# Retention scores as plain float32 products on halves and quarters of TensorE's array, with TensorE's order written by hand

## The chip, the cores and the metric

The kernel runs on one core of one Trainium2 chip. The metric is the time of one execution on the device, in microseconds (us); lower is better. Three runs of the kernel before were timed. A further execution was recorded by the hardware profiler, and all rows of the profile come from that one.

The engines by their names in the profile: PE is TensorE's matmul and PEld its weight load, DVE is VectorE, ACT is ScalarE, POOL is GpSimd, SP is SyncE, which here only issues transfers (its queue is SPq). L309 is line 309 of the kernel.

## The reference

Two stages follow each other: a causal retention over 8 batches of 576 tokens with 8 heads of width 64, and a layer of 8 experts in which each token goes to one.

```python
scores = scale * np.matmul(q, k.transpose(0, 1, 3, 2))
gamma = 1.0 - 2.0 ** (-5.0 - np.arange(H, dtype=np.float32))
rel = pos[:, None] - pos[None, :]
Dmat = np.where(rel >= 0, gamma[:, None, None] ** rel[None, :, :], 0.0)
attn = np.matmul(scores * Dmat[None], v)          # [8, 8, 576, 64]
x = attn.transpose(0, 2, 1, 3).reshape(4608, 512)
...
logits = x @ w_gate
e_idx = np.argmax(logits, axis=1)
for e in range(8):                                # only the tokens with e_idx == e
    h = np.maximum(x[mask] @ w1[e], 0.0)          # 512 -> 1024
    out[mask] = gate_w * eom * (h @ w2[e])        # 1024 -> 512
```

The largest logit decides the expert, so the retention's result has to be nearly exact float32.

## The kernel before, in words

The 4608 tokens are 36 tiles of 128. Nine tiles cover two batches, so the fifth of nine (c == 4) holds the end of one batch and the start of the next. Retention runs over these tiles with a running state: powers of gamma are multiplied into v (`vp`, on GpSimd) and into the output (`gq_sb`), so that the masked scores of a tile need only a mask of ones and zeros, and all earlier tiles of the batch enter through a state of 64x64 per head.

An iteration g of the main loop holds:

- `load`: one transfer of 1 MB brings q and k transposed, and k and v in natural order, into one of three buffers (`pk`). It is issued two tiles ahead, once the buffer is free.
- `update`: four matmuls over pairs of heads add this tile's k'v to `st_ps` (the two diagonal 64x64 blocks of a pair's 128x128 result are wanted), and ScalarE copies the diagonal blocks into `stbd`, whose other blocks are zero.
- `prep` for the next tile: `kh` (k cast to float32r, ScalarE) and `kl` (the difference, GpSimd), `qh` (two casts into block-diagonal arrays, ScalarE); `prep_ql` makes `ql` (two differences, VectorE).
- `scores`: per pair of heads three float32r products, kh'qh + kh'ql + kl'qh, each 128x128 by 128x256 over the block-diagonal q (L309). VectorE multiplies by the mask into `S_sb` (L311). The first tile alone (FP = 1) takes plain float32 products of 64 rows (L305).
- `xnat` of the tile before: four matmuls turn `xT` into natural order and give the gate logits in the same pass (L432); ScalarE copies x out, and SP writes it to `xs` in memory. After every fourth tile `gate1` runs the gating operations on VectorE and `gate2` ranks the tokens by two small matmuls; GpSimd then scatters slots into `lst`.
- `outT`: the state's product with q (L342, pairs of heads, block-diagonal state), then the values' product with `S_sb` (L347, one head at a time, 64 columns of the array), into `o_ps`; VectorE scales it into `xT` (L352).

The weights of expert 0 are loaded and cast in this loop too (`load_w`, L129 to L138). Near the end of the loop the first 384 slots of expert 0 are read and their tokens gathered and transposed; then the expert pass starts with `mm1` (L192) and goes on with `mm2` (L207) in an order written out by hand. In the retention loop a scheduler orders the instructions of each engine. Each engine runs its own list in that order and waits at semaphores for the others. PSUM has eight banks; here the scores have two tiles of two banks each.

Of the kernel before, what the change touches and what calls it, by code (L numbers as in the profile page):

```python
# [13 lines left out]
I32 = mybir.dt.int32  # L14
# [20 lines left out]
KB = DM // P  # L35
FB = F // P
GT = 4                      # tiles of a gating group
FP = 1                      # first tiles, whose scores are plain float32 products
NOV = 40                    # most overflow tiles
# [3 lines left out]
def tile_retention_moe(  # L43
# [44 lines left out]
    lists = const.tile([P, E, CT * 4, 2], I32, name="lists")   # (quadrant, j): slots of all column blocks  # L88
    idx = const.tile([P, E, CT, 2], I32, name="idx")           # by token column
    gidx = const.tile([P, E, CT * 4], I32, name="gidx")        # rows of a quarter of a token  # L90
# [4 lines left out]
    qbd = [[const.tile([P, NP, 2, P], F32R, name=f"q{x}{i}") for x in "hl"] for i in range(2)]  # L95
    stbd = [const.tile([P, NP, P], F32, name=f"stbd{i}") for i in range(2)]
# [50 lines left out]
    def gather_rows(e, t, rows):  # L147
        # From the first rows alone: an empty slot's index is beyond them and leaves its zeros.
        x = xg.tile([P, DM], F32, name="x_g")
        V.memset(x, 0.0)  # L150
        G.indirect_dma_start(out=x, out_offset=None, in_=xs[0:rows, :],
                             in_offset=bass.IndirectOffsetOnAxis(ap=idx[:, e, t, 0:1], axis=0),
                             bounds_check=rows - 1, oob_is_err=False)
        XG[e, t] = x

    def gather(e, t, u):
        # Quarter rows of 32 tokens, quarter a in partitions 32a on.
        if u == 0:
            XG[e, t] = pools["xq"].tile([P, 4, P], F32, name="x_q")
        G.indirect_dma_start(out=XG[e, t][:, u, :], out_offset=None, in_=xs.rearrange("t (a c) -> (t a) c", a=4),  # L160
                             in_offset=bass.IndirectOffsetOnAxis(ap=gidx[:, e, 4 * t + u:4 * t + u + 1], axis=0))
# [71 lines left out]
    actx = ExitStack()  # L233
    ld = actx.enter_context(tc.tile_pool(name="ld", bufs=3, side="right"))
# [3 lines left out]
    ps_s = psctx.enter_context(tc.tile_pool(name="ps_s", bufs=2, space=PSUM, side="right"))  # L238

    pk, ks, vs, xT, gt = {}, {}, {}, {}, {}  # L240
# [26 lines left out]
    def prep(g):  # L267
        c = g % CPB
        q = pk[g][:, 0].rearrange("p (a i) -> p a i", a=NP)
        k = pk[g][:, 1].rearrange("p (a i) -> p a i", a=NP)  # L270
        vp = wk.tile([P, H, D], F32, name="vp")
        vs[g] = vp
        if g < FP:
            G.tensor_tensor(out=vp, in0=pk[g][:, 3].rearrange("p (h d) -> p h d", h=H),
                            in1=gk_sb[:, c].broadcast_to([P, H, D]), op=ALU.mult)
            return
        kh = wk.tile([P, NP, P], F32R, name="kh")
        kl = wk.tile([P, NP, P], F32R, name="kl")
        A.copy(out=kh, in_=k)  # L279
        G.tensor_tensor(out=kl, in0=k, in1=kh.bitcast(F32), op=ALU.subtract)  # L280
        G.tensor_tensor(out=vp, in0=pk[g][:, 3].rearrange("p (h d) -> p h d", h=H),  # L281
                        in1=gk_sb[:, c].broadcast_to([P, H, D]), op=ALU.mult)
        ks[g] = (kh, kl)
        qh = qbd[g % 2][0]
        for r in range(2):
            s = slice(64 * r, 64 * r + 64)
            A.copy(out=qh[s, :, r, :], in_=q[s])  # L287

    def prep_ql(g):
        q = pk[g][:, 0].rearrange("p (a i) -> p a i", a=NP)  # L290
        qh, ql = qbd[g % 2]
        for r in range(2):
            s = slice(64 * r, 64 * r + 64)
            V.tensor_tensor(out=ql[s, :, r, :], in0=q[s], in1=qh[s, :, r, :].bitcast(F32), op=ALU.subtract)  # L294

    def scores(g):
        c = g % CPB
        sc = [ps_s.tile([P, 2, 2, P], F32, name=f"s{i}") for i in range(2)]
        S_sb = wk.tile([P, NP, 2, P], F32, name="S_sb", bufs=1)
        m = cmat_sb[:, 2 if c == 4 else 1, :, :].broadcast_to([P, 4, P])  # L300
        for p in range(NP):
            if g < FP:
                for r in range(2):
                    q, k = (pk[g][64 * r:64 * r + 64, i, P * p:P * p + P] for i in range(2))
                    T.matmul(sc[r][:, p // 2, p % 2], lhsT=k, rhs=q, start=True, stop=True)  # L305
                continue
            (kh, kl), (qh, ql) = ks[g], qbd[g % 2]
            for j, (a, b) in enumerate(((kh, qh), (kh, ql), (kl, qh))):
                T.matmul(sc[p // 2][:, p % 2], lhsT=a[:, p, :], rhs=b[:, p], start=(j == 0), stop=(j == 2))  # L309
        for i in range(2):  # L310
            V.tensor_tensor(out=S_sb[:, :, i] if g < FP else  # L311
                            S_sb[:, 2 * i:2 * i + 2].rearrange("p a r i -> p (a r) i"),
                            in0=sc[i].rearrange("p a r i -> p (a r) i"), in1=m, op=ALU.mult)
        return S_sb

    def update(g):
        c = g % CPB
        if c == 8:
            return
        if c in (0, 4):  # L320
            st_ps[0] = ps_1.tile([P, NP, P], F32, name="st_ps")
        lo = 64 if c == 4 else 0
        kn = pk[g][:, 2].rearrange("p (a i) -> p a i", a=NP)
        vv = vs[g].rearrange("p (a r) d -> p a (r d)", a=NP)
        for p in range(NP):
            T.matmul(st_ps[0][:, p, :], lhsT=kn[lo:P, p, :], rhs=vv[lo:P, p, :],
                     start=(c in (0, 4) and p == 0), stop=True, skip_group_check=True)
        s = stbd[g % 2]
        for r in range(2):
            q = slice(64 * r, 64 * r + 64)  # L330
            A.copy(out=s[q, :, q], in_=st_ps[0][q, :, q])
        stcur[0] = s

    def outT(g, S_sb, state):
        c = g % CPB
        o = ps_1.tile([P, NP, P], F32, name="o_ps")
        first = True
        q = pk[g][:, 0].rearrange("p (a i) -> p a i", a=NP)
        if state is not None:
            w = 64 if c == 4 else P  # L340
            for p in range(NP):
                T.matmul(o[:, p, 0:w], lhsT=state[:, p, :], rhs=q[:, p, 0:w],  # L342
                         start=first, stop=False, skip_group_check=True)
                first = False
        for p in range(NP):
            for r in range(2):
                T.matmul(o[64 * r:64 * r + 64, p, :], lhsT=vs[g][:, 2 * p + r, :],  # L347
                         rhs=S_sb[:, p, r, :], start=(state is None and p == 0), stop=True,
                         skip_group_check=True)
        x = wk.tile([P, NP, P], F32, name="xT", bufs=1)  # L350
        c0 = P * c if c < 5 else 64 + P * (c - 5)
        V.tensor_tensor(out=x, in0=o, in1=gq_sb[:, :, c0:c0 + P], op=ALU.mult)  # L352
# [40 lines left out]
    def gate2(ps, fresh):  # L393
# [20 lines left out]
        if n == SNAP:  # L414
            # Expert 0's first CA slots are read from here on: later tokens take slots from CA up.
# [36 lines left out]
    for t in stbd:  # L452
        V.memset(t, 0.0)
    for t in qbd[1] + qbd[0]:
        V.memset(t.bitcast(F32), 0.0)
    # The array's clock rises with work: zeros, while the first tile is on its way.
    warm = ps_1.tile([P, 512], F32, name="xa")
    for n in (512, 512, 256):
        T.matmul(warm[:, 0:n], lhsT=stbd[0][:, 0, :], rhs=stbd[0].rearrange("p a c -> p (a c)")[:, 0:n],
                 start=True, stop=True)  # L460
    prep(0)
    for g in range(NTILE):
        c = g % CPB
        if 0 < g < NTILE - 2:
            load(g + 2)
        prev = stcur[0] if c != 0 else None
        update(g)
        if g + 1 < NTILE:
            prep(g + 1)
        S_sb = scores(g)  # L470
# [4 lines left out]
        if FP <= g + 1 < NTILE:  # L475
            prep_ql(g + 1)
        outT(g, S_sb, prev)
        if g % 4 == 3 and g // 4 < 8:
            load_w(1 + (g // 4) % 2, 0, g // 8)
    psctx.close()  # L480
# [204 lines left out]
```

## Time and profile before

| | |
|---|---|
| time, median of 3 runs | 715.23 us (713.0 to 722.73) |
| span of the profiled execution | 718.8 us |
| instructions | 11429 |
| PE / PEld busy | 662.3 us (92%) / 598.4 us (83%) |
| DVE busy | 444.6 us (62%) |
| ACT busy | 226.3 us (31%) |
| POOL busy | 333.6 us (46%) |
| bytes moved | 103.60 MB, mean 144 GB/s |
| first L192 matmul (start of the expert pass) | 261.9 us |

The profiled execution's own time outside the profiler's span isn't among the numbers; its span is all that is used of it. The span runs from the first instruction to the last. A row of groups gives line, engine, operation, output and inputs, shapes and count, then the busy time, the mean duration in ns, and the idle time of the engine just ahead of it with what ended it. A row in order of time gives start, duration, engine, line and operation, and the count that was merged. In the table of stretches stand the stretch, its length, busy us and count of each engine, the granted clock of TensorE (1.00 is full), the mean busy share of the 16 DMA engines and GB/s.

### The profile page before, as it was taken

To read this page: it belongs to the slowest core of one execution; us is meant where nothing else is said; L and a number is where in the kernel's file an instruction comes from. 1 tells how busy PE (TensorE), PEld (TensorE's weight loads), DVE (VectorE), ACT (ScalarE), POOL (GpSimd) and SP (SyncE) were. 2 spreads that over 40 slices of the span, in tenths; PEclk is the share of its full clock that TensorE was granted. 3 is DMA by queue.
4 is the path that set the end of the run, shared out by engine and by line. 5 is a ranking of instruction groups with operands and counts; after the bars stand their busy time and mean duration, and the time that the engine had idled before them with its cause. 6 is when DMAs were issued, how large, how long until landed. Compare 5 with 4: busy or idle time off the path is not lost. (4 is left out here: it accounts for less than half of the span.)

```text
span 718.8 us, 11429 instructions
## 1 busy us (share of the span) xinstructions
PE 662.3 (92%) x4346; PEld 598.4 (83%) x4346; DVE 444.6 (62%) x836; ACT 226.3 (31%) x476; POOL 333.6 (46%) x305
## 2 busy tenths in 40 slices
PE   7988978798868799889999999999999999999996
PEld 5977877687767699769989989989989989988984
DVE  7778889997856862476765734744753753743500
ACT  4545554553434331222122222222222222222211
POOL 3353635644526423776716715724724733831011
PEclk9988999999989899999999999999999999999998
DMA  9867879758555511454513523622622722721000
GB/s 305 285 172 241 195 281 238 209 201 213 115 181 158 196 46 17 161 164 149 183 65 114 188 78 100 199 77 71 219 78 74 220 70 63 229 74 49 23 31 37
DMA packets 36762, 103.60 MB, mean 144 GB/s; under 512 B 10320, under 2 KB 13777, under 8 KB 32482
## 3 DMA queue, kind: packets, MB, share of 16 engines
q1 hardware_dynamic: 26946, 81.83, 37.6%
q0 software_dynamic: 9328, 19.98, 8.4%
q10 hardware_dynamic: 432, 1.05, 0.4%
q8 instruction: 35, 0.57, 0.4%
q14 instruction: 21, 0.17, 0.1%
HBM read 83.62 MB, written 20.26 MB: 145 GB/s over the span
## 5 line engine op out<-in xcount | busy, mean ns | idle before, releaser
L160 POOL DMA_INDIRECT x_q<-xs,gidx x148 | 167.8, 1134 | 54.8 <-issue 39.6
L192 PE MATMUL h_ps<-xh,w1h 128*128 128x384 f32 (+1 forms) x512 | 156.8, 307 | 4.4 <-DVE hl L195 3.0
L192 PE MATMUL h_ps<-xl,w1h 128*128 128x384 f32 (+1 forms) x512 | 157.0, 307 | 0.8 <-DVE xl L179 0.7
L192 PE MATMUL h_ps<-xh,w1l 128*128 128x384 f32 (+1 forms) x512 | 156.5, 306 | 0.0
L207 PE MATMUL y_ps<-w2h,hh 128*128 128x512 f32 x320 | 124.8, 390 | 1.5 <-ACT hh L194 1.5
L207 PE MATMUL y_ps<-w2h,hl 128*128 128x512 f32 x320 | 126.1, 394 | 0.0
L207 PE MATMUL y_ps<-w2l,hh 128*128 128x512 f32 x320 | 125.2, 391 | 0.0
L211 POOL DMA_INDIRECT out_dram<-y,idx x40 | 40.4, 1009 | 177.7 <-ACT y L210 161.0
L195 DVE SCALAR_TENSOR_TENSOR hl<-h_ps,hh 128x384 fp32r<-128x384 f32 (+1 forms) x128 | 60.6, 487 | 88.3 <-ACT hh L194 88.1
L194 ACT ACTIVATE hh<-h_ps 128x384 fp32r<-128x384 f32 (+1 forms) x128 | 55.8, 440 | 151.3 <-PE h_ps L192 148.9
L192 PEld LDWEIGHTS h_ps<-xh,w1h 128*128 128x128 f32 x512 | 96.0, 188 | 5.9 <-DVE hl L195 3.4
L192 PEld LDWEIGHTS h_ps<-xl,w1h 128*128 128x128 f32 x512 | 96.1, 188 | 1.8 <-DVE xl L179 1.5
L192 PEld LDWEIGHTS h_ps<-xh,w1l 128*128 128x128 f32 x512 | 96.1, 188 | 0.0
L294 DVE TENSOR_TENSOR ql<-pk,qh 64x512 fp32r<-64x512 f32 x70 | 69.3, 990 | 15.1 <-ACT qh L287 13.9
L179 DVE TENSOR_TENSOR xl<-x_t,xh 128x512 fp32r<-128x512 f32 x37 | 25.6, 692 | 75.9 <-ACT xh L178 75.9
L207 PEld LDWEIGHTS y_ps<-w2h,hh 128*128 128x128 f32 x320 | 60.1, 188 | 14.8 <-ACT hh L194 1.9
L207 PEld LDWEIGHTS y_ps<-w2l,hh 128*128 128x128 f32 x320 | 60.1, 188 | 13.5
L207 PEld LDWEIGHTS y_ps<-w2h,hl 128*128 128x128 f32 x320 | 60.1, 188 | 12.8 <-DVE hl L195 0.5
L347 PE MATMUL o_ps<-S_sb,vp 128*64 128x128 f32 x576 | 47.8, 299 | 24.5 <-DVE S_sb L311 24.4
L280 POOL TENSOR_TENSOR kl<-pk,kh 128x512 fp32r<-128x512 f32 x35 | 46.6, 1333 | 50.5 <-ACT kh L279 50.3
L210 ACT ACTIVATE y<-y_ps,idx 128x512 f32<-128x512 f32 x40 | 27.5, 688 | 129.8 <-issue 73.0
L281 POOL TENSOR_TENSOR vp<-pk,gk_sb 128x512 f32<-128x512 f32 x35 | 37.8, 1080 | 55.0 <-PE o_ps L347 23.7
(115 smaller groups left out, 1014.8 us busy)
## 6 DMA issues: line engine op xcount, KB each, us to landing
pk<-in_pack_dram SPq DMA_DIRECT2D x33, 1024.0 KB, 8.2
st<-in_w_dram SPq DMA_DIRECT2D x64, 512.0 KB, 4.2
xs<-x SPq DMA_DIRECT2D x36, 256.0 KB, 3.2
x_q<-xs,gidx POOLq DMA_INDIRECT x148, 3.3
pk<-in_pack_dram SPq DMA_DIRECT2D x3, 512.0 KB, 5.0
gq_sb<-in_gq_dram SPq DMA_DIRECT2D x5, 256.0 KB, 6.9
out_dram<-y,idx POOLq DMA_INDIRECT x40, 2.7
lst<-meta,sli POOLq DMA_INDIRECT x36, 5.8
```

The source lines that it names most:

```text
L160: G.indirect_dma_start(out=XG[e, t][:, u, :], out_offset=None, in_=xs.rearrange("t (a c) -> (t a) c", a=4), in_offset=bass.IndirectOffsetO ...
L179: V.tensor_tensor(out=lo, in0=src, in1=hi.bitcast(F32), op=ALU.subtract)
L192: T.matmul(ps, lhsT=a[:, k, :], rhs=b[:, k, :], start=(j == 0), stop=(j == 3 * KB - 1))
L194: A.activation(out=hh, in_=ps, func=AF.Relu)
L195: V.scalar_tensor_tensor(out=hl, in0=ps, scalar=0.0, in1=hh.bitcast(F32), op0=ALU.max, op1=ALU.subtract)
L207: T.matmul(ps, lhsT=a[:, n], rhs=b, start=(j == 0), stop=(j == 3 * FB - 1))
L210: A.activation(out=y, in_=ps, func=AF.Copy, scale=idx.bitcast(F32)[:, e, t, 1:2])
L211: G.indirect_dma_start(out=out, out_offset=bass.IndirectOffsetOnAxis(ap=idx[:, e, t, 0:1], axis=0), in_=y, in_offset=None, bounds_check=NT ...
L280: G.tensor_tensor(out=kl, in0=k, in1=kh.bitcast(F32), op=ALU.subtract)
L281: G.tensor_tensor(out=vp, in0=pk[g][:, 3].rearrange("p (h d) -> p h d", h=H), in1=gk_sb[:, c].broadcast_to([P, H, D]), op=ALU.mult)
L294: V.tensor_tensor(out=ql[s, :, r, :], in0=q[s], in1=qh[s, :, r, :].bitcast(F32), op=ALU.subtract)
L347: T.matmul(o[64 * r:64 * r + 64, p, :], lhsT=vs[g][:, 2 * p + r, :], rhs=S_sb[:, p, r, :], start=(state is None and p == 0), stop=True, sk ...
```

## The change

q and k are no longer split, and the block-diagonal arrays are gone. Scores are plain float32 products for all tiles, 64 rows of the array per head, the two heads of a pair into two banks. The state is kept as 64x64 blocks per head (`stT`); the state's product with q uses a quarter of the array per head, and the update uses 64 columns. The output's layout over partitions and banks changes with it, so the columns of x come in another order (`SLOT`); gate weights, w1 and `gq` are permuted to match ahead of the launch. There are four input buffers in place of three, three score banks used one at a time by two tiles, and two buffers for `S_sb`. TensorE's order in the loop is the order of the program text: scores of the next tile, `xnat` of the one before, `outT`, then `update`.

```diff
-FP = 1                      # first tiles, whose scores are plain float32 products
+SLOT = [[2 * (2 * (k % 2) + (c - k // 2) % 2) + k // 2 for c in range(2)] for k in range(4)]
...
-    qbd = [[const.tile([P, NP, 2, P], F32R, name=f"q{x}{i}") for x in "hl"] for i in range(2)]
-    stbd = [const.tile([P, NP, P], F32, name=f"stbd{i}") for i in range(2)]
+    zw = const.tile([P, 512], F32, name="zw")
+    stT = [const.tile([P, NP, D], F32, name=f"stT{i}") for i in range(2)]
...
-    ld = actx.enter_context(tc.tile_pool(name="ld", bufs=3, side="right"))
+    ld = actx.enter_context(tc.tile_pool(name="ld", bufs=4, side="right"))
...
-    ps_s = psctx.enter_context(tc.tile_pool(name="ps_s", bufs=2, space=PSUM, side="right"))
+    ps_s = psctx.enter_context(tc.tile_pool(name="ps_s", bufs=3, space=PSUM, side="right"))
...
     def prep(g):
...
-        kh = wk.tile([P, NP, P], F32R, name="kh")
-        kl = wk.tile([P, NP, P], F32R, name="kl")
-        A.copy(out=kh, in_=k)
-        G.tensor_tensor(out=kl, in0=k, in1=kh.bitcast(F32), op=ALU.subtract)
...
-            A.copy(out=qh[s, :, r, :], in_=q[s])
-
-    def prep_ql(g):
...
-            V.tensor_tensor(out=ql[s, :, r, :], in0=q[s], in1=qh[s, :, r, :].bitcast(F32), op=ALU.subtract)
+        vs[g] = wk.tile([P, H, D], F32, name="vp")
+        G.tensor_tensor(out=vs[g], in0=pk[g][:, 3].rearrange("p (h d) -> p h d", h=H),
+                        in1=gk_sb[:, g % CPB].broadcast_to([P, H, D]), op=ALU.mult)
 
     def scores(g):
-            for j, (a, b) in enumerate(((kh, qh), (kh, ql), (kl, qh))):
-                T.matmul(sc[p // 2][:, p % 2], lhsT=a[:, p, :], rhs=b[:, p], start=(j == 0), stop=(j == 2))
+        sc = [ps_s.tile([P, NP, P], F32, name="sc") for _ in range(2)]
+        S_sb = wk.tile([P, 2, NP, P], F32, name="S_sb")
+        for p in range(NP):
+            for r in range(2):
+                q, k = (pk[g][64 * r:64 * r + 64, i, P * p:P * p + P] for i in range(2))
+                T.matmul(sc[r][:, p], lhsT=k, rhs=q, start=True, stop=True)
         for r in range(2):
+            V.tensor_tensor(out=S_sb[:, r], in0=sc[r], in1=m, op=ALU.mult)
 
     def update(g):
-            st_ps[0] = ps_1.tile([P, NP, P], F32, name="st_ps")
+            st_ps[0] = ps_1.tile([P, NP, D], F32, name="st_ps")
         for p in range(NP):
-            T.matmul(st_ps[0][:, p, :], lhsT=kn[lo:P, p, :], rhs=vv[lo:P, p, :],
-                     start=(c in (0, 4) and p == 0), stop=True, skip_group_check=True)
-        s = stbd[g % 2]
-        for r in range(2):
-            q = slice(64 * r, 64 * r + 64)
-            A.copy(out=s[q, :, q], in_=st_ps[0][q, :, q])
+            for r in range(2):
+                o = P * p + 64 * r
+                T.matmul(st_ps[0][64 * r:64 * r + 64, p, :], lhsT=pk[g][lo:P, 2, o:o + D], rhs=vs[g][lo:P, 2 * p + r, :],
+                         start=(c in (0, 4) and p == 0), stop=True, skip_group_check=True)
+        A.copy(out=stT[g % 2], in_=st_ps[0])
 
     def outT(g, S_sb, state):
-        o = ps_1.tile([P, NP, P], F32, name="o_ps")
+        o = ps_s.tile([P, 2, 512], F32, name="o_ps", bufs=1)
+        part = lambda p, r: o[64 * ((p + r) % 2):64 * ((p + r) % 2) + 64, r, P * (p // 2):P * (p // 2) + P]
+        order = [(p, (p + i) % 2) for p in range(NP) for i in range(2)]
         if state is not None:
             w = 64 if c == 4 else P
-            for p in range(NP):
-                T.matmul(o[:, p, 0:w], lhsT=state[:, p, :], rhs=q[:, p, 0:w],
-                         start=first, stop=False, skip_group_check=True)
+            for p, r in order:
+                s = slice(64 * r, 64 * r + 64)
+                T.matmul(part(p, r)[:, 0:w], lhsT=state[s, p, :], rhs=pk[g][s, 0, P * p:P * p + w],
+                         start=(p < 2), stop=False, skip_group_check=True)
+        for p, r in order:
+            T.matmul(part(p, r), lhsT=vs[g][:, 2 * p + r, :], rhs=S_sb[:, r, p, :],
+                     start=(state is None and p < 2), stop=True, skip_group_check=True)
...
     prep(0)
+    pe_order = tc.manual_schedule(engines={mybir.EngineType.PE})
+    pe_order.__enter__()
+    S_next = scores(0)
     for g in range(NTILE):
-        if 0 < g < NTILE - 2:
-            load(g + 2)
-        prev = stcur[0] if c != 0 else None
-        update(g)
+        S_sb = S_next
+        prev = stcur[0] if g % CPB != 0 else None
+        if g < NTILE - 3:
+            load(g + 3)
         if g + 1 < NTILE:
             prep(g + 1)
-        S_sb = scores(g)
+            S_next = scores(g + 1)
...
         if g > 0:
             xnat(g - 1)
-        if FP <= g + 1 < NTILE:
-            prep_ql(g + 1)
         outT(g, S_sb, prev)
+        update(g)
         if g % 4 == 3 and g // 4 < 8:
             load_w(1 + (g // 4) % 2, 0, g // 8)
+    pe_order.__exit__(None, None, None)
```

More of the change, by code (lines that the diff above doesn't have):

```diff
@@ L237, in tile_retention_moe @@
     ps_1 = p1ctx.enter_context(tc.tile_pool(name="ps_1", bufs=1, space=PSUM))
-    ps_s = psctx.enter_context(tc.tile_pool(name="ps_s", bufs=2, space=PSUM, side="right"))
-    pk, ks, vs, xT, gt = {}, {}, {}, {}, {}
+    ps_s = psctx.enter_context(tc.tile_pool(name="ps_s", bufs=3, space=PSUM, side="right"))
+    pk, vs, xT, gt = {}, {}, {}, {}
     st_ps, stcur = [None], [None]
@@ L267, in prep @@
     def prep(g):
[L268 to L276, printed above, removed]
-        kh = wk.tile([P, NP, P], F32R, name="kh")
-        kl = wk.tile([P, NP, P], F32R, name="kl")
@@ L279, in prep @@
[L279 to L284, printed above, removed]
-        for r in range(2):
-            s = slice(64 * r, 64 * r + 64)
-            A.copy(out=qh[s, :, r, :], in_=q[s])
-    def prep_ql(g):
-        q = pk[g][:, 0].rearrange("p (a i) -> p a i", a=NP)
-        qh, ql = qbd[g % 2]
-        for r in range(2):
-            s = slice(64 * r, 64 * r + 64)
-            V.tensor_tensor(out=ql[s, :, r, :], in0=q[s], in1=qh[s, :, r, :].bitcast(F32), op=ALU.subtract)
@@ L296, in scores @@
[L296 to L300, printed above, removed]
-        for p in range(NP):
[L302 to L307, printed above, removed]
-            for j, (a, b) in enumerate(((kh, qh), (kh, ql), (kl, qh))):
[L309 to L313, printed above, removed]
+        vs[g] = wk.tile([P, H, D], F32, name="vp")
@@ new lines, in prep, with scores @@
+        G.tensor_tensor(out=vs[g], in0=pk[g][:, 3].rearrange("p (h d) -> p h d", h=H),
+                        in1=gk_sb[:, g % CPB].broadcast_to([P, H, D]), op=ALU.mult)
+    def scores(g):
+        sc = [ps_s.tile([P, NP, P], F32, name="sc") for _ in range(2)]
+        S_sb = wk.tile([P, 2, NP, P], F32, name="S_sb")
+        m = cmat_sb[:, 2 if g % CPB == 4 else 1, :, :].broadcast_to([P, NP, P])
+        for p in range(NP):
+            for r in range(2):
+                q, k = (pk[g][64 * r:64 * r + 64, i, P * p:P * p + P] for i in range(2))
+                T.matmul(sc[r][:, p], lhsT=k, rhs=q, start=True, stop=True)
+        for r in range(2):
+            V.tensor_tensor(out=S_sb[:, r], in0=sc[r], in1=m, op=ALU.mult)
@@ L320, in update @@
         if c in (0, 4):
-            st_ps[0] = ps_1.tile([P, NP, P], F32, name="st_ps")
+            st_ps[0] = ps_1.tile([P, NP, D], F32, name="st_ps")
         lo = 64 if c == 4 else 0
-        kn = pk[g][:, 2].rearrange("p (a i) -> p a i", a=NP)
-        vv = vs[g].rearrange("p (a r) d -> p a (r d)", a=NP)
         for p in range(NP):
-            T.matmul(st_ps[0][:, p, :], lhsT=kn[lo:P, p, :], rhs=vv[lo:P, p, :],
-                     start=(c in (0, 4) and p == 0), stop=True, skip_group_check=True)
@@ L328, in update @@
-        s = stbd[g % 2]
-        for r in range(2):
-            q = slice(64 * r, 64 * r + 64)
-            A.copy(out=s[q, :, q], in_=st_ps[0][q, :, q])
-        stcur[0] = s
+            for r in range(2):
[3 more added lines that the diff above has]
+        A.copy(out=stT[g % 2], in_=st_ps[0])
@@ L334, in outT @@
+        stcur[0] = stT[g % 2]
     def outT(g, S_sb, state):
         c = g % CPB
-        o = ps_1.tile([P, NP, P], F32, name="o_ps")
-        first = True
-        q = pk[g][:, 0].rearrange("p (a i) -> p a i", a=NP)
+        o = ps_s.tile([P, 2, 512], F32, name="o_ps", bufs=1)
+        part = lambda p, r: o[64 * ((p + r) % 2):64 * ((p + r) % 2) + 64, r, P * (p // 2):P * (p // 2) + P]
+        order = [(p, (p + i) % 2) for p in range(NP) for i in range(2)]
         if state is not None:
             w = 64 if c == 4 else P
-            for p in range(NP):
-                T.matmul(o[:, p, 0:w], lhsT=state[:, p, :], rhs=q[:, p, 0:w],
-                         start=first, stop=False, skip_group_check=True)
-                first = False
@@ L345, in outT @@
[L345 to L349, printed above, removed]
+            for p, r in order:
+                s = slice(64 * r, 64 * r + 64)
+                T.matmul(part(p, r)[:, 0:w], lhsT=state[s, p, :], rhs=pk[g][s, 0, P * p:P * p + w],
+                         start=(p < 2), stop=False, skip_group_check=True)
@@ L350, in outT @@
+        for p, r in order:
+            T.matmul(part(p, r), lhsT=vs[g][:, 2 * p + r, :], rhs=S_sb[:, r, p, :],
+                     start=(state is None and p < 2), stop=True, skip_group_check=True)
         x = wk.tile([P, NP, P], F32, name="xT", bufs=1)
         c0 = P * c if c < 5 else 64 + P * (c - 5)
-        V.tensor_tensor(out=x, in0=o, in1=gq_sb[:, :, c0:c0 + P], op=ALU.mult)
+        V.tensor_tensor(out=x.rearrange("p (r s) i -> p r s i", r=2),
+                        in0=o[:, :, 0:2 * P].rearrange("p r (s i) -> p r s i", s=2),
+                        in1=gq_sb[:, :, c0:c0 + P].rearrange("p (r s) i -> p r s i", r=2), op=ALU.mult)
@@ L451, in tile_retention_moe @@
     load_first()
[L452 to L455, printed above, removed]
+    V.memset(zw, 0.0)
     warm = ps_1.tile([P, 512], F32, name="xa")
     for n in (512, 512, 256):
-        T.matmul(warm[:, 0:n], lhsT=stbd[0][:, 0, :], rhs=stbd[0].rearrange("p a c -> p (a c)")[:, 0:n],
-                 start=True, stop=True)
+        T.matmul(warm[:, 0:n], lhsT=zw[:, 0:P], rhs=zw[:, 0:n], start=True, stop=True)
     prep(0)
+    pe_order = tc.manual_schedule(engines={mybir.EngineType.PE})
+    pe_order.__enter__()
+    S_next = scores(0)
     for g in range(NTILE):
-        c = g % CPB
-        if 0 < g < NTILE - 2:
-            load(g + 2)
-        prev = stcur[0] if c != 0 else None
-        update(g)
+        S_sb = S_next
+        prev = stcur[0] if g % CPB != 0 else None
+        if g < NTILE - 3:
+            load(g + 3)
         if g + 1 < NTILE:
             prep(g + 1)
-        S_sb = scores(g)
+            S_next = scores(g + 1)
         if g < 4:
@@ L634, in _consts @@
     gqh = gam[:, None] ** s[None, :] / np.sqrt(D)
-    gq = np.repeat(gqh.reshape(NP, 2, 1, 640), D, axis=2).reshape(NP, P, 640).transpose(1, 0, 2)
+    gq = np.repeat(gqh[np.array(SLOT)][:, :, None], D, axis=2).reshape(NP, P, 640).transpose(1, 0, 2)
     pos = (np.arange(CPB)[None, :] * P + np.arange(P)[:, None]) % S
@@ L666 @@
     tr = lambda a: nat(a).reshape(NTILE, P, NP, P).transpose(0, 3, 2, 1).reshape(NTILE, P, DM)
+    perm = (np.array(SLOT).reshape(-1, 1) * D + np.arange(D)).reshape(-1)
     arrays = {
         "pack": np.ascontiguousarray(np.stack([tr(q), tr(k), nat(k), nat(v)], axis=2)),
-        "wg": np.concatenate([inputs["moe_w_gate"], inputs["moe_w_output_gate"]], axis=1),
-        "w1": np.ascontiguousarray(np.asarray(inputs["moe_w1"]).reshape(E, P, KB, 4, 256)
+        "wg": np.ascontiguousarray(np.concatenate([inputs["moe_w_gate"], inputs["moe_w_output_gate"]], axis=1)[perm]),
+        "w1": np.ascontiguousarray(np.asarray(inputs["moe_w1"])[:, perm].reshape(E, P, KB, 4, 256)
                                    .transpose(0, 3, 1, 2, 4).reshape(E, 4, P, KB * 256)),
```

## The prediction

> **What bounds the kernel now.** I read the page's head first, then the table of busy time by stretches, then the list of waits, then the order of time of single tiles.
>
> ```profile
> span 718.8 us, 11429 instructions
> core 0: us, PE busy (x) PEld busy (x) DVE busy (x) ACT busy (x) POOL busy (x), PEclk, DMA share, GB/s
> 0.00:40.00 40.00, 34.69 (x292) 29.67 (x292) 29.65 (x69) 20.83 (x44) 15.16 (x20) 1.00 0.88 305
> 40.00:120.00 80.00, 67.31 (x561) 61.51 (x560) 65.89 (x138) 39.72 (x85) 39.02 (x35) 0.89 0.76 205
> 120.00:200.00 80.00, 68.11 (x584) 61.57 (x585) 70.16 (x153) 36.13 (x81) 39.28 (x34) 0.94 0.70 196
> 200.00:264.00 64.00, 50.90 (x423) 46.55 (x423) 44.66 (x117) 26.01 (x61) 28.16 (x25) 0.89 0.47 159
> 320.00:718.80 398.80, 391.05 (x2208) 354.58 (x2206) 206.85 (x299) 92.27 (x181) 179.78 (x160) 1.00 0.34 109
> ...
> L192 PEld LDWEIGHTS h_ps<-xh,w1h x40: 186/188/190, 261.9 to 299.9; 128*128 128x128 f32 x40
> ...
> 9.73 0.33 SPq L245 DMA_DIRECT2D pk<-in_pack_dram  x1
> ...
> 235.49 0.33 SPq L245 DMA_DIRECT2D pk<-in_pack_dram  x1
> ...
> DMA to landing us min/median/max: 4.9/8.2/12.0
> ...
> ACT kh L279 <- DMA pk<-in_pack_dram: 49.7, 18, 7.2
> PE o_ps L347 <- DVE S_sb L311: 24.4, 16, 5.6
> ```
>
> The expert pass is TensorE alone (391 of 399 us busy, full clock), and the change does not touch it. Its first product (L192) starts at 261.9, so what the change can move is the time of that start, the handover. Before it no engine is full: TensorE has gaps, its granted clock falls to 0.89, and VectorE and the DMA engines are half to nine tenths busy. What sets the pace is a loop. The loads of tiles 3 and 35 are issued at 9.73 and 235.49, so 32 tiles take 225.8 us, **7.06 us a tile**. There are three input buffers. A load takes 8.2 us to land; only then do the cast of k (which waits 49.7 us for it in all), the casts of q, the two differences, the scores, the masking and the output products run, and only after them is the buffer free for the tile three further on. Three periods are 21.2 us: 8.2 of load and 13 of work and waits in series.
>
> **The change part by part.** TensorE first. Each matmul on float32 shows as two weight loads and two matmuls, here called pairs.
>
> ```profile
> 229.38 0.97 PEld L326 LDWEIGHTS st_ps<-vp,pk 128*128 128x128 f32 x8 [0.17 <-issue]
> 230.27 0.19 PEld L309 LDWEIGHTS s<-qh,kh 128*128 128x128 f32 x1
> ...
> 231.55 0.19 PEld L309 LDWEIGHTS s<-qh,kl 128*128 128x128 f32 x1
> 251.88 0.55 PEld L432 LDWEIGHTS xa<-iw,xT 128*128 128x128 f32 x4
> 252.37 0.56 PEld L432 LDWEIGHTS xb<-iw,xT 128*128 128x128 f32 x4
> 252.86 0.98 PEld L342 LDWEIGHTS o_ps<-pk,stbd 128*128 128x128 f32 x8
> 253.96 0.85 PEld L347 LDWEIGHTS o_ps<-S_sb,vp 128*64 128x64 f32 x16
> ...
> 5.51 0.97 PEld L305 LDWEIGHTS s<-pk 64*128 64x128 f32 x16 [0.33 <-DMA pk<-in_pack_dram]
> ...
>   issue: 4.6, 22
> ```
>
> Taking off one load's own length, a full-array pair comes every 0.111 us (L326: 0.97 less 0.19, over 7 steps) or 0.113 us (L342); the split scores every 0.116 us (1.28 us over 11 steps); the return to natural order (L432) takes 0.49 us for four, 0.98 us in all. Where the array is split, two run side by side: column halves (L347) come every 0.048 us, row halves (L305, the first tile's plain scores) every 0.052 us. The last row is L326's idle time for which nothing was waited, between 40 and 240 us: 4.6 us in 22 cases, 0.21 us at each return from column halves to the full array. L347 starts 1.10 us after L342, of which the 8 pairs explain 0.90, so the way in costs 0.2 us as well.
>
> Before, a tile needs 8 x 0.111 (state) + 12 x 0.116 (scores) + 0.98 + 8 x 0.113 (state's output) + 16 x 0.048 (values) + 2 x 0.2 = **5.3 us**, 192 us for 36 tiles. After, the scores are 16 row-half pairs, 16 x 0.052 = 0.83; L432 stays 0.98; the values stay 0.76. The state's output becomes 16 quarter pairs and the state 16 column-half pairs with 64 moving columns. Neither is in the trace. From the nearest rows they cost no more than a half-array pair (16 x 0.052 = 0.83 each); half of that, 0.42, if quarters run four at a time and 64 columns take half of 128. I take the upper end, since the only concurrency seen is two. The shape changes four times in a tile (row halves, full, quarters, column halves, row halves): 0.8 us. The sum is **4.2 to 5.0 us**, taken as 5.0, 180 us for 36 tiles: 0.3 us (0.3 to 1.1) off TensorE's own work in a tile, 11 to 40 us in all. That alone would be little.
>
> The Trainium skill, TensorEngine Tiling, section Tiling Modes, says that changing the tiling mode, not just the tile, drains TensorE; that speaks against this change, which doubles such changes. The 0.2 us measured above agrees with it; without the rule the sum would be 0.8 us a tile lower. The Trainium skill, TensorE: Matmul & The Clock Gate, section "Wait — 56ns, not 53.3ns?", says that matmuls never start closer than about 25 ns; if weight loads count in the same way, an estimate from that figure is 50 ns a pair, and quarters would win nothing over halves. No row here shows a quarter.
>
> Then what else goes, and the rest of the chain.
>
> ```profile
> L294 DVE TENSOR_TENSOR ql<-pk,qh 64x512 fp32r<-64x512 f32 x70 | 69.3, 990 | 15.1 <-ACT qh L287 13.9
> L311 DVE TENSOR_TENSOR S_sb<-s,cmat_sb 128x512 f32<-128x512 f32 x72 | 47.5, 681 | 7.2 <-PE s L309 6.7
> L352 DVE TENSOR_TENSOR xT<-o_ps,gq_sb 128x512 f32<-128x512 f32 x36 | 24.6, 684 | 9.7 <-PE o_ps L347 9.6
> L287 ACT CAST qh<-pk 64x512 fp32r<-64x512 f32 x70 | 43.0, 615 | 0.9
> L331 ACT COPY stbd<-st_ps 64x256 f32<-64x256 f32 x64 | 23.4, 366 | 40.6 <-PE st_ps L326 39.7
> L279 ACT CAST kh<-pk 128x512 fp32r<-128x512 f32 x35 | 21.7, 619 | 50.0 <-DMA pk<-in_pack_dram 49.7
> L280 POOL TENSOR_TENSOR kl<-pk,kh 128x512 fp32r<-128x512 f32 x35 | 46.6, 1333 | 50.5 <-ACT kh L279 50.3
> ```
>
> VectorE is busy 210 us before 264 us (the four stretches added); 69.3 of the q differences go and 141 remain, 3.9 us a tile. ScalarE has 122.7, and loses 43.0 + 21.7 and half of L331's 23.4 (one copy in place of two; 0.37 us stays if it costs what the halves did): 46. GpSimd has 121.6 and loses 46.6: 75. None of these three can then set the pace alone. The six removed instructions of a tile and their handoffs also leave the stretch between landing and scores: cast of k 0.62, casts of q 1.23, difference of k 1.33, about 3.2 us if each is waited for, which TensorE feels because today it has no score tile in hand. After, raw loads feed the scores one tile ahead, so the masking (2 x 0.68 us) lies beside the return (0.98) and the products of the tile before (about 2.4); its 24.4 us of waits should go. What is late next: the eviction of xT (0.68) now has only the state update and the next scores (1.3 to 1.7 us) as cover ahead of L432. If VectorE is in the gating operations then, TensorE stands, and since its order is fixed, output products, update and scores stand behind it.
>
> The gating operations of a group take, in one instance,
>
> ```profile
> 236.98 0.19 DVE L360 TENSOR_REDUCE mx<-lg 128x4 f32<-128x32 f32 x1
> ...
> 239.18 2.97 DVE L374 TENSOR_TENSOR cum<-c,oh 128x8 bf16<-128x8 bf16 x1
> ...
> L133 ACT CAST w2h<-st 128x1024 fp32r<-128x1024 f32 x4 | 4.2, 1047 | 2.9 <-DMA st<-in_w_dram 2.8
> ...
> st<-in_w_dram SPq DMA_DIRECT2D x8, 512.0 KB, 7.4
> ```
>
> 5.2 us from the first to the end of the running count. Nine such groups could each hold TensorE for nothing (a tile period passes before it asks for them) up to 5 us, 0 to 45 us; I take 1 us, 9 in all. The casts of expert weights are in ScalarE's queue ahead of the state's copy and of x: today the four of w2 wait 2.8 us for their loads; if each of the 8 waited a whole landing (7.4) it would be 59. I take 2 us each, 16, half of it beside TensorE's work. The added load per iteration is none: the loads are the same 36, only issued one tile earlier, and behind a load that waits on SP for its buffer stands only the write of x, for which no tile of this stage waits. The removed clearings at the start (two of VectorE's at 0.91 us after the first products) lie beside the first load; I cost them at nothing.
>
> **The buffers.** With four, a load is issued at the end of tile g-1's update and its scores come two iterations later, so two periods must hold one landing: 8.2 us gives 4.1 us a tile, the worst landing (12.0) 6.0. So the loop no longer sets 7.06, and the DMA engines themselves do:
>
> ```profile
> 8.00:12.00 4.00, 2.56 (x27) 2.21 (x28) 1.09 (x5) 2.30 (x5) 2.75 (x3) 1.00 1.07 355
> 84.00:88.00 4.00, 3.53 (x30) 3.36 (x30) 2.68 (x5) 1.58 (x4) 1.93 (x3) 1.00 0.99 58
> ```
>
> The busy shares of the first four stretches give 0.88 x 40 + 0.76 x 80 + 0.70 x 80 + 0.47 x 64 = **182 us** of DMA work before the handover, and none of it is removed. It isn't all bytes: at 84 us the engines were fully busy and moved 58 GB/s, where 8 to 12 us show 355. Such stretches recur after the scatters of a group; I can't see why, and keep them.
>
> **The sum.** DMA: 182 us less some 6 behind the last load is 176; at the opening's share of 0.88 to 1.0 the last load lands at 4 + 176 to 200 = 180 to 204 us, against some 242 now (235.49 and a landing of 4.9 to 8.2). Two tiles, the last return and the transposes follow, some 13 us (20 now): handover at 193 to 217. TensorE: 5.5 (L305's start) + 180 + 9 + 8 (half of the casts' 16) + some 3 of transposes = 206. Both come out alike, so I take 207: **55 us earlier** than 261.9, 5.6 us a tile. The expert pass keeps its length. The profiled span of 718.8 becomes 664; it lies 0.5% over the median of the three runs (715.23), and the same 55 us off the median give 660.
>
> **Rivals.** (a) The DMA stalls fade or overlap, and quarters run four at a time: TensorE at 4.2 us plus 0.3 of waits, 5.5 + 36 x 4.5 + 8 = 175, so 628. For: the share exceeds 1.0 in stretches; against: no quarter is measured, and the stalls recur with the scatters. (b) Fixed order turns each late eviction, gating chain or weight cast into a TensorE wait: at the upper ends above (45 and 59, not all together) about 27 us more than forecast, handover 234, 687. For: VectorE's 2.97 us operation above shows that a short one can take long; against: the two largest waits shown, for the load and for S_sb, are those that the change takes from TensorE's path. (c) Nothing measurable: DMA stalls lengthen with two loads in flight and the period stays at 6.8 us, 9 us less in all, 706. Against: the first 40 us run at 305 GB/s. (d) Slower: tiles that differ in both row and column half do not run side by side, and neither do the scores. All 48 pairs of scores, state and its output then cost a full pair, 0.116: 5.6 + 0.98 + 0.76 + 0.8 = 8.1 us a tile, 36 x 1.07 = 39 us later than 7.06, 754. It decides from a mean pair of 0.094 us ((7.06 - 2.54) / 48); L305 and L347 at 0.052 and 0.048 speak against it.
>
> **How the numbers follow.** Forecast 0.62 (about 640 to 680), (a) 0.15, (b) 0.15, (c) 0.05, (d) 0.03. The range takes in most of (a) and (b): 631 to 691. The kernel can be told from no change by about 2%, 14 us; so faster 0.92, same 0.05, slower 0.03.
>
> **What would show it.** The first L192 product near 207; loads issued every 5 to 6 us; waits of TensorE for S_sb nearly gone; DMA share over 0.85 from 40 to 180 us; 16 weight loads of the state's output in 0.4 to 0.85 us; ScalarE near 46 us before the handover. It would be wrong if loads were still spaced by 6.5 us or more, if TensorE waited for xT or gating in every tile, or if quarters took 0.1 us a pair.

## The result: 3% faster, less than half of what was forecast

The changed kernel takes 695.0 us (median of 4, 691.24 to 697.93) against 718.38 us (4 runs) for the kernel before: a ratio of 0.9685, 95% interval 0.9633 to 0.9737. That is 23 us off where 55 were forecast, and 695 lies over the range's 691. The profiled span is 691.2 us, 27.6 less than before. Two repetitions of the changed kernel, e0 and e11 below, gave 0.9700 and 0.9770.

The table of stretches up to the start of the expert pass (columns as before: busy us and count of each engine, granted clock, DMA share, GB/s), of the kernel before:

```profile
0.00:262.00 262.00, 219.13 (x1848) 197.73 (x1848) 208.57 (x466) 121.94 (x268) 121.62 (x113) 0.92 0.69 207
```

and of the changed kernel, with the first product of the expert pass, the loads, and the waits of TensorE by their releasers (total us, times, longest):

```profile
0.00:234.00 234.00, 185.36 (x2498) 159.74 (x2499) 123.64 (x391) 50.67 (x131) 73.22 (x78) 0.86 0.80 232
...
L193 PEld LDWEIGHTS h_ps<-xh,w1h x512: 186/188/335, 234.0 to 656.3; 128*128 128x128 f32 x171
...
L246 SPq DMA_DIRECT2D pk<-in_pack_dram x33: 327/328/892, 8.5 to 207.5; - x33
DMA to landing us min/median/max: 6.9/9.4/12.2
...
PE sc L281 <- DMA pk<-in_pack_dram: 16.3, 9, 3.6
PE xa L401 <- DVE xT L319: 11.3, 6, 6.0
PE xb L365 <- DVE lg L411: 7.8, 8, 1.8
PE sc L281 <- DVE S_sb L283: 4.9, 1, 4.9
PE xa L401 <- DVE es L355: 3.6, 1, 3.6
```

The handover moved from 261.9 to 234.0, 27.9 us; the expert pass kept its 457. VectorE, ScalarE and GpSimd fell to 124, 51 and 73 us, near the 141, 46 and 75 worked out. Now split the time up to the handover into TensorE's idle time, its busy time at full clock (busy x granted clock), and the rest, which the clock took:

| | before | after |
|---|---|---|
| handover | 262 | 234 |
| idle | 43 | 49 |
| busy x clock | 202 | 159 |
| lost to the clock | 17 | 26 |

TensorE's own work fell by 42 us, far more than the 12 I had put down. But idle time rose by 6 and the clock took 9 more. The waits above, with four small ones, come to the same 49 us.

Where nothing waits, a tile takes 4.35 us, from scores to scores (order of time, the changed kernel):

```profile
193.91 1.16 PE L281 MATMUL sc<-pk 64*128 64x128 f32 x16
...
198.26 1.16 PE L281 MATMUL sc<-pk 64*128 64x128 f32 x16
```

36 of these are 157 us. What much of the other 77 is made of can be seen in one place. Order of time, changed kernel:

```profile
82.10 1.16 PE L281 MATMUL sc<-pk 64*128 64x128 f32 x16
...
86.02 1.04 ACT L134 CAST w2h<-st 128x1024 fp32r<-128x1024 f32 x1 [5.98 <-DMA st<-in_w_dram]
...
87.10 0.69 DVE L139 TENSOR_TENSOR w2l<-st,w2h 128x512 fp32r<-128x512 f32 x1 [6.79 <-ACT w2h L134]
...
88.39 0.69 DVE L319 TENSOR_TENSOR xT<-o_ps,gq_sb 128x512 f32<-128x512 f32 x1
...
89.22 1.06 PE L401 MATMUL xa<-iw,xT 128*128 128x144 f32 x3 [5.96 <-DVE xT L319]
...
95.17 1.16 PE L281 MATMUL sc<-pk 64*128 64x128 f32 x16
```

A weight tile lands late, ScalarE stands 5.98 us at its cast, VectorE stands 6.79 us at the split behind the cast, the eviction of xT is queued behind the split, and TensorE stands 5.96 us. Then, by stretches:

```profile
80.00:84.00 4.00, 3.26 (x65) 2.82 (x64) 0.30 (x2) 0.04 (x1) 1.04 (x1) 1.00 0.86 65
84.00:88.00 4.00, 0.00 (x0) 0.00 (x0) 0.90 (x3) 1.59 (x3) 0.00 (x0) 1.00 0.79 299
88.00:92.00 4.00, 2.78 (x20) 2.53 (x24) 2.52 (x6) 0.84 (x3) 0.00 (x0) 0.53 0.82 281
```

Ahead of the gap the DMA engines are 0.86 busy and move only 65 GB/s. Behind it the granted clock is 0.53: from L401 to the next scores TensorE takes 5.95 us (89.22 to 95.17), where the tile before took 3.27 (78.83 to 82.10). The input buffer comes free late with it: the next load is issued at 95.33, 6.65 us after the one at 88.68. The second such place is the reading of expert 0's list:

```profile
194.05 0.33 SPq L246 DMA_DIRECT2D pk<-in_pack_dram  x1
204.30 0.33 SPq L218 DMA_DIRECT2D lists<-lst  x1
...
205.94 0.15 DVE L230 COPY idx<-lists 32x6 int32<-32x6 int32 x1 [7.34 <-DMA lists<-lst]
206.15 0.35 SPq L246 DMA_DIRECT2D pk<-in_pack_dram  x1
...
207.90 2.07 PE L281 MATMUL sc<-pk 64*128 64x128 f32 x14 [4.85 <-DVE S_sb L283]
```

L218 stands on SP for 9.7 us until the scatters have landed, and the last two input loads stand behind it; VectorE stands 7.34 us at the copy of the list, with the masking of scores behind it.

### The profile page after: what moved, and what is told of

It reads as the page before. It is cut to its first block, busy times and chain, and to the rows that moved or that the text cites. A ratio compares the mean times of both kernels' runs of the same rounds, so it can differ in the third digit from the quotient of the medians.

```text
span 691.2 us, 12360 instructions
## 1 busy us (share of the span) xinstructions
PE 629.9 (91%) x4998; PEld 561.9 (81%) x4998; DVE 359.2 (52%) x761; ACT 155.3 (22%) x339; POOL 284.6 (41%) x270
## 5 line engine op out<-in xcount | busy, mean ns | idle before, releaser
L281 PE MATMUL sc<-pk 64*128 64x128 f32 x576 | 49.3, 315 | 21.2 <-DMA pk<-in_pack_dram 16.3
L180 DVE TENSOR_TENSOR xl<-x_t,xh 128x512 fp32r<-128x512 f32 x37 | 25.6, 693 | 75.5 <-ACT xh L179 75.5
L281 PEld LDWEIGHTS sc<-pk 64*128 64x128 f32 x576 | 41.4, 214 | 25.5 <-DMA pk<-in_pack_dram 15.9
L376 POOL DMA_INDIRECT lst<-meta,sli x36 | 35.5, 986 | 61.7 <-DVE sli L374 45.0
L283 DVE TENSOR_TENSOR S_sb<-sc,cmat_sb 128x512 f32<-128x512 f32 x72 | 46.4, 684 | 25.8 <-PE sc L281 25.7
```

The costliest lines, as they stand in the source:

```text
L180: V.tensor_tensor(out=lo, in0=src, in1=hi.bitcast(F32), op=ALU.subtract)
L281: T.matmul(sc[r][:, p], lhsT=k, rhs=q, start=True, stop=True)
L283: V.tensor_tensor(out=S_sb[:, r], in0=sc[r], in1=m, op=ALU.mult)
L376: i = G.indirect_dma_start(out=lst, out_offset=bass.IndirectOffsetOnAxis(ap=sli[:, t, :], axis=0), in_=meta[:, t, :], in_offset=None)
```

## Experiments

Two theories: **T**, the transfers (loads, and slow stretches behind the scatters) hold the pace, and TensorE could go at 4.1 us; **O**, the fixed order holds it, with late operations at the head of the line. Each ratio is to the kernel before as timed beside that run. It took 708 to 710 us beside most of them, but 751 beside e9 and e10, whose expert passes were longer too (495 and 535 us, where the others', but for e1 with its other routing, took 456 to 464). A start of the expert pass comes from one profiled execution; the changed kernel's own was 234.0 above and 227.7 and 227.8 in e0 and e11, so a few us between two starts can't be read.

**e1: only four tiles loaded.**

```diff
-        if g < NTILE - 3:
+        if g == 0:
             load(g + 3)
+        elif g < NTILE - 3:
+            pk[g + 3] = pk[(g + 3) % 4]
```

> The changed kernel, but only the first four tiles are loaded (from tile 4 on each tile reuses the buffer of the tile four before, so all later tiles compute on the first four tiles' q, k and v; routing and the end of the kernel differ, and only the start of the expert pass is read). All else stays: writes of x, scatters, weight loads, TensorE's order. Theory T (transfers): the loads and waits for landings set the pace, TensorE's own tile is about 4.1 us; the first L193 product then comes at 165 to 185 us (234 in the changed kernel) and DMA busy share falls under 0.4. Theory O (fixed order): TensorE waits mostly because xT, gating and weight splits are late in its fixed order; only the 16 us of waits for loads go, and the first L193 product comes at 210 to 220.

```profile
L193 PEld LDWEIGHTS h_ps<-xh,w1h x512: 186/188/192, 193.8 to 614.0; 128*128 128x128 f32 x171
0.00:194.00 194.00, 168.64 (x2500) 145.80 (x2501) 120.43 (x392) 51.06 (x131) 73.51 (x78) 0.95 0.33 107
```

193.8: 34 to 40 us earlier than the three starts of the changed kernel, nearer to T, though outside both bands. Busy x clock is 160, the same work; idle is 25 and the clock takes 8. In the changed kernel idle time was 44 to 49 us and the clock took 22 to 26 (e0, e11 and the table above). So the loads cost 18 to 23 us of waiting and 13 to 18 us of clock, and 25 us of waits are there without them.

**e4: no scatters in the first seven groups** (`if n > SNAP:` ahead of the line that queues them).

> The changed kernel without the scatters of slots of the first seven gating groups (28 of 36 indirect writes of 128 x 8 bytes; the lists then hold empty slots, so most expert tiles gather a row of zeros and write nothing; only the time up to the expert pass is read). If the stretches with DMA engines busy and little moved come from the scatters, the DMA busy work before the expert pass falls from about 190 us to 140 to 150, and the pass starts at 200 to 215. If they come from something else, DMA work stays over 175 us and the start at 225 to 235.

```profile
0.00:199.00 199.00, 169.19 (x2496) 146.32 (x2497) 119.98 (x391) 50.64 (x130) 45.66 (x50) 0.93 0.76 269
...
DMA to landing us min/median/max: 4.7/7.1/11.5
```

Start at 199.3, 28 to 35 us earlier, with the same loads, just under the first band. DMA work is 0.76 x 199 = 151 us against 0.80 x 234 = 187 (182 in e0 and e11); the median landing falls from 9.4 to 7.1 us. Cut into 4 us each from 28 to 196 us, the changed kernel has ten stretches in which the engines are at least 0.7 busy and move less than 200 GB/s; this kernel has none. So those stretches do come from the scatters, and cost 31 to 36 us of DMA work. GpSimd is spared the 28 instructions as well (73 to 46 us busy), but that isn't it: TensorE stood only 0.2 us for `vp` in the changed kernel, and e10 keeps these instructions.

**e10: each slot in 64 bytes of its own.**

```diff
-    lst = dram.tile([E * NT, 2], I32, name="lst")
+    lst = dram.tile([E * NT, 16], I32, name="lst")
...
+        V.tensor_scalar(out=sli, in0=slf, scalar1=8.0, scalar2=None, op0=ALU.mult)
```

> The changed kernel with each slot of the list in a row of 64 bytes of its own (8 bytes before), so that the 8-byte writes of a scatter don't lie next to each other; the clearing of the list grows to 2.4 MB (some 6 us of DMA work), and reading it takes longer behind the start of the expert pass, so only the time up to there is read. If neighbouring small writes cause the slow stretches, DMA work up to the start falls from about 184 to 150 to 165 us and the start comes at 200 to 215. If it is the scatters as such, work stays over 180 and the start at 226 to 240.

```profile
L193 PEld LDWEIGHTS h_ps<-xh,w1h x512: 186/188/338, 214.5 to 714.5; 128*128 128x128 f32 x171
0.00:214.50 214.50, 175.16 (x2499) 149.06 (x2499) 120.51 (x391) 49.94 (x131) 73.80 (x78) 0.94 0.77 263
```

Start at 214.5, at the top of the band, with all scatters in place. DMA work up to there is 0.77 x 214.5 = 165 us, some 6 of it the larger clearing, against 182 to 187 in the changed kernel and 151 without the scatters (e4); of the ten slow stretches one is left. So most of the DMA work that the scatters cost goes when their small writes no longer lie next to each other. As a kernel it gains nothing (one run, 751.72 us; the kernel before 751.24).

**e3: three input buffers** (`bufs=3`, `load(g + 2)`).

> The changed kernel with three input buffers and loads two tiles ahead, as before the change. Theory T: a load is issued when the tile before the last is released and is wanted one iteration later, so one period must hold one landing (9.4 us median): 7 to 9 us a tile, expert pass starts at 255 to 300, total 715 to 755, no better than before the change. Theory O: the input buffers don't matter, the start stays within 10 us of 234, total near 695.

```profile
PE sc L281 <- DMA pk<-in_pack_dram: 46.2, 20, 5.3
```

707.42 us, ratio 0.9987 (0.9941 to 1.0033), start at 245.6, 12 to 18 us later than with four: the products without the fourth buffer gain nothing. The start is earlier than T said (255), the total missed its band by 8 us.

**e7: the kernel before with deeper loads** of q and k.

```diff
+        pk[g] = ld.tile([P, 2, 512], F32, name="pk", bufs=4)
+        SP.dma_start(out=pk[g], in_=pack[g, :, 0:2])
...
+        pn[g] = ld.tile([P, 2, 512], F32, name="pn", bufs=3)
```

> The kernel before the change with q and k loaded three tiles ahead into four buffers (k and v in natural order stay two ahead in three; the gathered rows have two buffers in place of three to make room). Theory T: the wait for the load was the head of its loop, so most of the change's gain comes without its products: casts wait less for pk, expert pass starts 15 to 30 us before that of the kernel before, total at 0.96 to 0.98. Rival: the splits and their handoffs set its pace, and depth alone gives under 7 us (0.99 to 1.01).

```profile
120.00:200.00 80.00, 68.86 (x627) 63.72 (x628) 74.45 (x172) 42.61 (x95) 42.81 (x37) 0.98 0.89 239
...
PE xa L437 <- DVE xT L357: 11.6, 6, 4.5
```

Ratio 1.0026 (0.9944 to 1.0108): T fell here. The start is 250.2, but the kernel before took 709.7 us beside this run, not 718; with an expert pass of 457 us its own start would be near 251 (an estimate, it wasn't profiled there). ScalarE's wait for pk falls from 49.7 to 7.0 us, but VectorE is busy 74.45 of 80 us. So in the kernel before, the load loop wasn't the only limit: depth alone (e7) and the new products alone (e3) gain nothing, both together 16 to 23 us. That the second limit is the splitting on VectorE is read from its busy share, not shown by a run of its own.

**e5: the scheduler's order for TensorE** (the two lines around the loop taken out).

> The changed kernel without the hand-written order of TensorE (the scheduler orders it, as before the change; program text unchanged). Theory T: the same transfers, so the expert pass starts within 10 us of 234, total 685 to 705. Theory O: without head-of-line waits TensorE runs ahead, start at 205 to 222, total 665 to 683.

681.37 us, ratio 0.9584 (0.9504 to 0.9664), start at 222.0, at the edge of O's band. The changed kernel again, **e0**, is at 0.9700 (0.9616 to 0.9784), start 227.7; once more, **e11**, at 0.9770 (0.9723 to 0.9816), a little over what was expected, start 227.8. The hand order is no gain. Whether it costs the 6 us between the starts isn't settled: e5's interval meets e0's and lies under e11's, and neither was timed beside e5.

> The changed kernel again, as the control for the other three of this call: 0.9685 of the kernel before within 0.01, the expert pass starts at 225 to 236.

> The changed kernel once more, as the control for e9 and e12: the kernel before was slower in e9's call (751 us), so its ratio has to be taken beside the changed kernel's. 0.965 to 0.975 of the kernel before, start of the expert pass 225 to 236.

**e6: order by hand on four engines, with the weight casts and the list's reading moved back.**

```diff
-    pe_order = tc.manual_schedule(engines={mybir.EngineType.PE})
+    pe_order = tc.manual_schedule(engines={ET.PE, ET.Activation, ET.DVE, ET.SP})
...
+        if g == 32:
+            load_idx(0, 1, 0)
...
+        if g in casts:
+            cast_w(*casts.pop(g))
         if g % 4 == 3 and g // 4 < 8:
-            load_w(1 + (g // 4) % 2, 0, g // 8)
+            casts[g + 2] = (1 + (g // 4) % 2, 0, g // 8, load_st(1 + (g // 4) % 2, 0, g // 8))
```

> The changed kernel with the order of ScalarE, VectorE and SP in the retention loop also written by hand (program order), the weight casts of expert 0 two tiles behind their loads, the gating behind the eviction of xT and its ranking one tile later, and the reading of expert 0's list behind the last input load. Theory T says the rest is transfers: waits of TensorE for xT and S_sb (about 20 us in the changed kernel, and the half clock behind them) go, those for pk grow, expert pass starts at 205 to 220, total 15 to 28 us under the changed kernel. Theory O (the loss is mostly operations that wait for a landing at the head of an engine's order) says 195 to 207. If neither, 225 or more.

```profile
PE sc L288 <- DMA pk<-in_pack_dram: 28.8, 12, 3.8
...
PE xa L405 <- DVE xT L326: 0.3, 1, 0.3
```

684.06 us, ratio 0.9651 (0.9581 to 0.9722), start at 225.2, neither theory's band: the waits for xT are gone, those for the loads took their place. Neither total nor start can be told from e0, which was timed beside it.

**e8: a fifth input buffer** (`bufs=5`, `load(g + 4)`).

> The changed kernel with a fifth input buffer and loads four tiles ahead. Theory T: the DMA engines are 0.85 to 0.9 busy with four, so there is little left: waits of TensorE for pk fall from 16 us to under 8, total 0 to 12 us under the changed kernel. If landings were still the limit and not the engines' work, 15 to 30 us under it.

```profile
PE xa L401 <- DVE xT L319: 16.5, 7, 5.4
...
PE sc L281 <- DMA pk<-in_pack_dram: 2.4, 2, 2.0
```

The mirror image, as T said: waits for pk gone, those for xT stay. Ratio 0.9681 (0.9600 to 0.9762), start at 223.7, nor can this be told from e0.

**e9 and e12: both at once, and the same with four buffers.** The diffs are those of e6 and e8; the gather of expert 0 comes one tile earlier.

> The kernel of e6 (hand order on four engines, casts behind their loads) with five input buffers as in e8, and the gather of expert 0's rows one tile earlier. e6 alone left TensorE 28.8 us of waits for pk, e8 alone left 16.5 us for xT; if these two waits only covered for each other, both go now: expert pass starts at 205 to 216, total 0.945 to 0.96 of the kernel before. If the DMA engines' work (about 184 us with the stretches behind the scatters) is the floor, the start stays at 218 to 228 and the total at 0.96 to 0.97.

> e9 with four input buffers in place of five. If the waits for loads and the waits for operations behind a landing cover for each other, the fifth buffer is needed: start at 218 to 228, 0.96 to 0.968 of the kernel before (e6's). If the earlier gather is what e9 gained, start at 208 to 216, 0.945 to 0.958.

```profile
L200 PEld LDWEIGHTS h_ps<-xh,w1h x512: 186/188/330, 212.2 to 671.8; 128*128 128x128 f32 x171
0.00:212.00 212.00, 179.97 (x2497) 152.77 (x2498) 125.63 (x391) 49.25 (x130) 72.68 (x78) 0.94 0.81 256
...
PE xa L405 <- DVE xT L326: 7.5, 8, 3.1
...
PE sc L288 <- DMA pk<-in_pack_dram: 2.6, 2, 2.0
```

These rows are e9's. The stretch up to the start of e12:

```profile
0.00:223.60 223.60, 183.47 (x2498) 158.05 (x2499) 127.07 (x391) 50.55 (x131) 72.47 (x78) 0.88 0.81 243
```

e9 starts its expert pass at 212.2, the earliest of the kernels with all their transfers, and has the lowest ratio, 0.9525 (0.9461 to 0.9590): some 36 us under the kernel before beside it. Its interval meets those of e5 and e12, so the total alone doesn't part it from them. e12 is at 0.9618 (0.9570 to 0.9666), with its start at 223.6 and 25.6 us of waits for pk, near e6. Split as above:

| | e12, four buffers | e9, five buffers |
|---|---|---|
| start of the expert pass | 224 | 212 |
| idle | 40 | 32 |
| busy x clock | 161 | 169 |
| lost to the clock | 22 | 11 |

The earlier gather is in both, so it isn't what e9 gained. The two waits covered for each other: the order alone leaves 28.8 us for pk (e6), the fifth buffer alone 16.5 us for xT (e8), both together 2.6 and 7.5. That takes 8 us of idle time and 11 us of lost clock off e12. The 11 us between the two starts isn't a clean measure of it: e9 ran on another chip than e12 and beside a slower kernel before, and its products took 8 us longer.

## Why the prediction was wrong

**What held.** The expert pass didn't move. The work of VectorE, ScalarE and GpSimd came out within an eighth of the sums (141, 46, 75 forecast; 124, 51, 73 measured). The direction was right. The fourth buffer took TensorE's waits for input loads from 46.2 us (e3) to 16.3, and TensorE's waits for S_sb fell from 24.4 to 4.9. Loads followed each other by 4.3 us where nothing stood in the way (146.02 to 150.31), but by 6.2 us on average (8.54 to 207.54, 32 loads), over the 5 to 6 that were to show it.

**TensorE's products: two terms mis-sized.** I took 0.83 us each for the 16 quarter pairs and the 16 of the update, the upper of two bounds. Order of time:

```profile
152.43 0.42 PEld L312 LDWEIGHTS o_ps<-pk,stT 64*64 64x64 f32 x16
152.44 0.67 PE L312 MATMUL o_ps<-pk,stT 64*64 64x128 f32 x16
...
153.85 0.60 PEld L297 LDWEIGHTS st_ps<-vp,pk 128*64 128x64 f32 x16
154.52 0.97 PEld L281 LDWEIGHTS sc<-pk 64*128 64x128 f32 x16
```

Sixteen quarter matmuls, 0.269 us each by their median, start within 0.40 us: one every 0.027 us, four side by side, half of what I took. With the 64-column update at (0.60 - 0.14) / 15 = 0.031 us, the tile is 4.35 us, near the lower end of 4.2 to 5.0. The Trainium skill, TensorE: Matmul & The Clock Gate, section "Wait — 56ns, not 53.3ns?", has 25 ns as the closest start of two matmuls; 27 ns agrees with it, and weight loads don't count towards it here. This error would have made the kernel faster than forecast.

**The sum of waits: the step that failed.** I set the handover at the larger of two sums that came out alike, 206 by TensorE and 193 to 217 by the DMA engines, as if each ran at its own pace beside the other. The DMA sum counted on the opening's share of 0.88 to 1.0 and on a last load landing at 180 to 204; the share up to the handover was 0.80, and the last load was issued at 207.5. TensorE's sum has 17 us of waits (9 and 8), 189 us of all else, and nothing for the clock. Measured were 49, 159 and 26. So waits and clock were 58 us over the sum, and the quicker products hid 30 of them.

Of the 49 us, waits for xT and the gating are 24.6, not far over the 17 forecast. The 16.3 for input loads and the 4.9 behind the list's reading stood in TensorE's sum at nothing:

- I wrote that behind a load on SP "stands only the write of x". The weight loads and the reading of the list stand in that queue too, and the list's reading stands ahead of the last two input loads. It did so before the change:

```profile
230.91 1.26 SPq L217 DMA_DIRECT2D lists<-lst  x3
...
SPq L217 <- DMA lst<-meta,sli: 8.8, 1, 8.8
```

- The weight casts I put at 16 us on ScalarE, half hidden. ScalarE's waits for weights were 13.6 us, so the size was near. But the wait passes on to VectorE and from there to xT: one chain, four engines, above.
- The slow stretches I kept as DMA work, rightly, but took the average for the pace. Four buffers let a load be wanted two tiles after its issue, 8.7 us at 4.35 a tile; the landings took 9.4 us in the median and up to 12.2.

**The clock: a term left out.** I read 0.89 to 0.94 from the first table and gave it no price. Behind the gap of 5.96 us the granted clock was 0.53, and a shorter wait was enough too: these sixteen scores, behind 2.63 us, took 2.08 us in place of 1.16.

```profile
34.74 2.08 PE L281 MATMUL sc<-pk 64*128 64x128 f32 x16 [2.63 <-DMA pk<-in_pack_dram]
```

So a wait of some us costs more than itself, 26 us of 234 in all. The Trainium skill, TensorE: Matmul & The Clock Gate, section "What's actually happening", says that after an idle window of about 3.4 us the clock passes 4 of 8 pulses; the granted 0.50 to 0.53 behind the gaps agrees, but the row above shows that a wait under 3.4 us can be enough. Why the clock took more than before, 26 against 17, fits the length of the waits: before, one wait of TensorE reached 3.5 us (5.6, for S_sb); after, four did (5.96, 4.85, 3.60 and 3.55).

**The reading of the loop: half right.** I took depth for what set the 7.06 us. e7 shows that another limit stood at the same height, by the busy share the splitting on VectorE. The change removed both, so this didn't cost the forecast anything, but a change to one of the two would have been forecast wrongly.

**Rival (b): the right number by luck.** Late operations at the head of a line gave 234 and 687, and the handover was 234.0. But its mechanism, 27 us more of waits for evictions, gating and casts, measured only 8 us more (24.6 against 17); loads and clock made up the rest, and quicker products hid part of it. Repeated, the handover was 227.7 and 227.8, and without the fixed order (e5) it was 222.0.

## What to carry to other kernels

When two engines' sums come out alike, don't take the larger: bursts on one become gaps on the other, and on TensorE a gap of a few us is paid again in part by the lower clock behind it (here 26 us on 49 us of waits). Before pricing a deeper prefetch, list every instruction in each in-order queue that waits for a transfer to land, also those that belong to other work (weight casts, list reads), and follow what is queued behind it. If removing one wait gains nothing and another takes its place, remove both in one kernel before calling it a floor.

## What the runs showed of the hardware

- 28 indirect writes of 128 x 8 bytes, 29 KB in all, cost 31 to 36 us of the DMA engines' time and 28 to 35 us of the kernel; the 1 MB loads beside them land in 9.4 us, and in 7.1 without them. With each slot in 64 bytes of its own most of the DMA time is gone. Why neighbouring small writes do this, the runs don't show.
- Quarters of the array in both directions run four side by side: 0.027 us a matmul of 128 columns, against 0.048 to 0.052 on halves and 0.111 on the full array.
- A wait of TensorE of 2.63 us was followed by products at about half speed (2.08 us where 1.16 is usual).
- The change from quarters to column halves costs TensorE 0.2 us (L315's idle time for which nothing was waited: 5.4 us in 27 cases), which agrees with the Trainium skill, TensorEngine Tiling, section "Tiling Modes", that a change of tiling mode drains TensorE.
